# A fused attention and mixture-of-experts kernel: later issue points for the first pass's factors, and the first expert's last 640 tokens cut as 384 and 256

## The chip, the cores and the metric

The kernel runs on one core of a Trainium2 chip (trn2). The metric is the device time in microseconds (us) of one execution of the whole program; lower is better. Its engines run side by side, each through its own queue in order: PE multiplies matrices, DVE, ACT and POOL do elementwise work, SP issues the transfers (DMA).

## The reference

Three layers follow each other. Attention has 4 batches of 8 heads, 576 positions and a mask by blocks of 64. Its output, 2304 tokens of 512 numbers, goes through 8 experts, weighted by a gate whose exponentials are normalised eight times by rows and by columns. The last layer is a dense one with a soft activation and a layer norm.

```python
logits = x @ w_gate
logits = logits - logits.max()
P = np.exp(logits)
for _ in range(8):
    P /= P.sum(1, keepdims=True) + 1e-09
    P /= P.sum(0, keepdims=True) + 1e-09
    P *= N / E
out = np.zeros((N, D), dtype=np.float32)
for e in range(E):
    h = np.maximum(x @ w1[e], 0.0)
    ye = h @ w2[e]
    out += P[:, e:e + 1] * ye
```

## The kernel before

All products are made of pairs of rounded high and low parts, so that one product is three matrix multiplications. The work has these stages:

- **Attention**, up to about 370 us. Products of the first expert (units 0 and 1, half an expert each) are mixed into it as fill. The tokens of the first expert come in segments of 512 and 640; for each block `first_expert` runs the gate (L386 to L396, which writes `logits`), then unit by unit a first layer (L533 to L535, PSUM tile `hps`, from which ACT makes a high half `h` at L539 and DVE a low half at L540) and a second layer (L569 to L571, `yps`). The tiles `hps` and the gate's tiles share two PSUM buffers.
- **The handover**, about 370 to 450 us. The last segment of 640 tokens (`begun`) is still to be done, now in turn with the normalisation of the gate. `sinkhorn` gives ten steps: an exponential (L409), eight rounds (L417 to L431, almost all on DVE, with one small product `cs` at L425 on PE in the middle), and a transposed copy. In the loop of ten, each step is followed by at least 20 units of cost of `begun`. Two steps of `spread_x` (L597 on ACT, L599, L611 to L618) make the sums of token blocks, `X`, for the first pass, and `first_factors(2, ...)` makes the weight factors `W` of unit 2: seven splits, each a cast on ACT (L445) and a subtraction on POOL (L446), and sums of raw weights on DVE (L656, L657, L658, L664).
- **Pass 0**, about 450 to 865 us: units 2 to 15 on the first 768 tokens, with seven products instead of eight for a first layer (`psa`, `psb`, `psc`, L708 to L710; sums at L720, `h` at L750 and L751) and a second layer (L862 to L864, added to `acc` at L868). Each unit also makes the next unit's factors and second weights (`second_weights`, L673, L690 to L700), and from unit 10 on DVE decodes weights of the last layer (L465 to L483).
- **Passes 1 and 2**, to about 1770 us, and then the last layer.

The order of each engine's instructions is not that of the code. A scheduler of the framework takes the place in the code as priority and puts ahead what it thinks could start earlier, so an edit at one place can shift rows hundreds of microseconds later. On the machine each engine then keeps to its list, and a row that waits holds up all rows behind it.

Of the kernel before, what the change touches and what calls it, by code (L numbers as in the profile page):

```python
# [24 lines left out]
def build(ctx, tc, qT, kT, v, w_gate, w1, w1s, w2, w_in, w_out, g_ln, out):  # L25
# [356 lines left out]
    def gate(x, t0, w, t):  # L382

        ps = mm.tile([P, 512], F32, tag="mm", name="gps")
        for n, (c, s) in enumerate([(c, s) for c in range(4) for s in (1, 0)]):
            nc.tensor.matmul(ps[:, 0:w], gw[:, c, :], x[s][:, c, t0 : t0 + w], start=n == 0, stop=n == 7)  # L386
        lt = stg.tile([P, 512], F32, tag="raw", name="glt")[0:64, 0:w]
        nc.scalar.copy(lt, ps[0:64, 0:w])
        yield 9
        pt = mm.tile([P, 4, 64], F32, tag="mm", name="gpt")  # L390
        k = w // P
        for j in range(k):
            nc.tensor.transpose(pt[:, j, :], lt[:, j * P : j * P + P], ident[0:64, 0:64])
        lg = logits[:, t : t + k, :]
        nc.vector.tensor_copy(lg, pt[:, 0:k, 0:E])
        nc.vector.tensor_tensor(lg, pt[:, 0:k, 32 : 32 + E], lg, op=ALU.add)  # L396
        yield 0
# [97 lines left out]
    def load_first(u, pool):  # L495
        e, g = divmod(u, 2)
        wts[u] = ([], [])
        for c in range(4):
            wts[u][0].append(load_weight(pool, w1[e, 4 * g + c]))
            yield 0  # L500

    def load_second(u, pool):
        e, g = divmod(u, 2)
        for c in range(4):
            wts[u][1].append(load_weight(pool, w2[e, (4 * g + c) * P : (4 * g + c + 1) * P, :]))
            yield 0
# [131 lines left out]
    def first_factors(u, stg):  # L638

        e, g = divmod(u, 2)  # L640
        W = {}

        def split(i, a):
            t = weight_tile()
            split_weights(t, a)
            nc.sync.dma_start(fdram[u - 2, int(i) - 1], r32(t))
            W[i] = by_halves(t)

        raw = {}
        for i, k in ((1, 1), (2, 1), (2, 2), (1, 2)):  # L650
            raw[i, k] = stg.tile([P, 512], F32, tag="raw", name="raw")
            nc.sync.dma_start(raw[i, k], w1s[e - 1, g, i - 1, k - 1])
        a11, a12, a21, a22 = raw[1, 1], raw[1, 2], raw[2, 1], raw[2, 2]
        s1 = stg.tile([P, 512], F32, tag="s1", name="s1", bufs=1)
        split("1", a11)
        nc.vector.tensor_tensor(s1, a21, a22, op=ALU.add)  # L656
        nc.vector.tensor_tensor(a21, a11, a21, op=ALU.subtract)  # L657
        nc.vector.tensor_tensor(a11, s1, a11, op=ALU.subtract)  # L658
        split("6", a11)
        split("2", a12)  # L660
        split("7", a21)
        split("5", s1)
        split("4", a22)
        nc.vector.tensor_tensor(a12, a12, a11, op=ALU.subtract)  # L664
        split("3", a12)
        return W
# [212 lines left out]
    def woven(job, other, first, every):  # L879

        for i, cost in enumerate(job):
            yield cost
            if i >= first and (i - first) % every == 0:
                next(other, None)
        run(other)

    def first_expert(seg, tile0, u, v):

        x = xseg[seg]
        blocks = ((0, 512),) if seg == 0 else ((0, 256), (256, 384))  # L890
        for t0, w in blocks:
            yield from gate(x, t0, w, tile0 + t0 // P)
        for i, (t0, w) in enumerate(blocks):
            job = moe(u, x, t0, w, tile0 + t0 // P, "first")
            if i == len(blocks) - 1:
                yield from woven(job, load_first(v, w1p), 17, 3)
            else:
                yield from job
        for i, (t0, w) in enumerate(blocks):
            job = moe(v, x, t0, w, tile0 + t0 // P, "second")  # L900
            yield from woven(job, load_second(v, w1p), 2, 3) if i == 0 else job


    fills = [
        [12, 12 + 9, 9, (1 for _ in load_unit(0, w1p))],
        [44, 80, 200, first_expert(0, 0, 0, 1)],
        [80, 116, 270, first_expert(1, 4, 1, 0)],
        [116, 157, 200, first_expert(0, 9, 0, 1)],
    ]
    done = [0] * len(fills)  # L910
# [30 lines left out]
    W = None  # L941
    for i in range(10):
        next(rounds)
        if i in (1, 5):
            next(spreading)
        if i == 3:
            W = first_factors(2, stg2)
        cost = 0
        while cost < 20:
            cost += next(begun, 20)  # L950
# [231 lines left out]
```

## Time and profile before

| | us |
|---|---|
| median of 3 runs | 1983.65 |
| lowest and highest run | 1982.28, 1986.76 |
| profiled execution, its own time | 1983.74 |
| its span in the trace | 1982.0 |
| PE busy | 1898.4 |
| DVE busy | 1454.0 |
| POOL busy | 1163.6 |
| ACT busy | 743.3 |

The span is the stretch that the trace covers; 1.7 us of the execution's own time lie around it. Busy time of PE counts a pipelined matrix multiplication up to its modelled end. A row of a timeline gives a start, a duration, the engine, the line, the operation, the tiles (out<-in), the shape and, in brackets, how long the engine had been idle before it and who ended that.

### The profile page before, as it was taken

The numbers are of one execution on the slowest core, as the hardware profiler recorded it, in microseconds if no ns is written. First come the engines' busy times: TensorE is split into PE (matmuls) and PEld (weight loads), VectorE is DVE, ScalarE is ACT, GpSimd is POOL, SyncE is SP. The second block draws the span as 40 slices with busy tenths as digits, with TensorE's granted clock in tenths as the row PEclk, the third lists the DMA queues.
The fourth block names the chain that finished last, engine by engine and source line by source line (L and its number), as shares of the span: only waits on it lengthen the run. The fifth ranks groups of instructions, "written<-read, shape, count | busy, mean of one in ns | idle before, by whom it ended". The sixth has DMA issues, their size and how long they took to land.

```text
span 1982.0 us, 31143 instructions
## 1 busy us (share of the span) xinstructions
PE 1898.4 (96%) x10487; PEld 1762.7 (89%) x10487; DVE 1454.0 (73%) x3104; ACT 743.3 (38%) x1555; POOL 1163.6 (59%) x920
## 2 busy tenths in 40 slices
PE   5899999889999999999999999998999999989999
PEld 4688998788998989889999999987999999978887
DVE  5868677666777769888867667797866766678774
ACT  5766657433434434343222222222222122224332
POOL 7775645455766667656666676668757557631000
PEclk8999999999999999999999999998999999989999
DMA  8765554337888888879787787876788787851100
GB/s 233 189 181 150 153 148 117 134 99 270 298 303 309 292 315 311 297 251 370 271 289 265 272 279 257 288 259 238 282 285 294 257 278 274 307 205 44 47 28 32
DMA packets 197758, 454.61 MB, mean 229 GB/s; under 512 B 20432, under 2 KB 78432, under 8 KB 197472
## 3 DMA queue, kind: packets, MB, share of 16 engines
q1 hardware_dynamic: 197600, 452.63, 67.3%
q8 instruction: 84, 1.38, 0.3%
q14 instruction: 74, 0.61, 0.1%
HBM read 295.72 MB, written 128.52 MB: 214 GB/s over the span
## 4 chain that ended last, share of the span: by engine, by line
PE 77%; DVE 9%; DMA 4%; POOL 4%; issue 3%; ACT 1%; SPq 1%; DVEq 0%; POOLq 0%; ACTq 0%
PE yps L708 5%; PE yps L710 5%; PE yps L709 5%; PE psb L709 4%; PE psb L708 4%; PE psb L710 4%; PE yps L862 3%; PE yps L864 3%; PE yps L863 3%; PE psc L710 2%; PE psc L708 2%; PE psc L709 2%; PE psa L708 2%; PE psa L710 2%; PE psa L709 2%
## 5 line engine op out<-in xcount | busy, mean ns | idle before, releaser
L770 POOL TENSOR_TENSOR hf<-hb,hf 128x768 fp32r<-128x768 f32 x196 | 368.4, 1895 | 94.9 <-ACT hf L769 94.9
L769 ACT CAST hf<-hb 128x768 fp32r<-128x768 f32 x196 | 160.5, 836 | 490.4 <-POOL hb L773 158.5
L708 PE MATMUL yps<-hf,W 128*128 128x384 f32 x784 | 268.1, 342 | 10.5 <-DVE hb L762 8.2
L709 PE MATMUL yps<-hf,W 128*128 128x384 f32 x784 | 267.1, 341 | 0.0
L710 PE MATMUL yps<-hf,W 128*128 128x384 f32 x784 | 263.8, 341 | 0.0
L773 POOL TENSOR_TENSOR hb<-hb 128x768 f32<-128x768 f32 x84 | 158.8, 1891 | 161.6 <-DVE hb L762 160.1
L816 DVE TENSOR_TENSOR acc<-yps,acc 128x384 f32<-128x384 f32 x364 | 192.6, 549 | 67.6 <-PE yps L710 66.9
L446 POOL TENSOR_TENSOR w<-raw,w 128x512 fp32r<-128x512 f32 x96 | 125.8, 1323 | 109.3 <-ACT w L445 104.6
L708 PE MATMUL psb<-X,W 128*128 128x384 f32 x504 | 169.7, 337 | 1.4 <-ACT acc L814 1.4
L709 PE MATMUL psb<-X,W 128*128 128x384 f32 x504 | 169.3, 336 | 0.0
L710 PE MATMUL psb<-X,W 128*128 128x384 f32 x504 | 167.7, 335 | 0.0
L708 PEld LDWEIGHTS yps<-hf,W 128*128 128x128 f32 x784 | 149.0, 190 | 13.1 <-DVE hb L762 9.8
L709 PEld LDWEIGHTS yps<-hf,W 128*128 128x128 f32 x784 | 149.1, 190 | 0.0
L720 DVE TENSOR_TENSOR u<-psb,r 128x384 f32<-128x384 f32 x168 | 91.1, 550 | 79.1 <-PE psb L710 71.4
L710 PEld LDWEIGHTS yps<-hf,W 128*128 128x128 f32 x784 | 148.7, 190 | 0.0
L862 PE MATMUL yps<-w,h 128*128 128x512 f32 x336 | 133.3, 397 | 5.5 <-DVE acc L868 2.7
L233 POOL TENSOR_SCALAR e<-e,sv 128x128 f32<-128x128 f32 (+2 forms) x144 | 81.1, 567 | 95.6 <-DVE sv L229 31.4
L446 POOL TENSOR_TENSOR W<-raw,W 128x512 fp32r<-128x512 f32 x84 | 117.7, 1416 | 29.7 <-ACT W L445 29.7
L864 PE MATMUL yps<-w,h 128*128 128x512 f32 x336 | 132.6, 395 | 0.0
L863 PE MATMUL yps<-w,h 128*128 128x512 f32 x336 | 132.5, 394 | 0.0
L1102 POOL TENSOR_SCALAR lh<-ln 128x1024 f16<-128x1024 f32 x18 | 19.1, 1059 | 187.4 <-DVE ln L1099 65.2
L708 PE MATMUL psa<-X,W 128*128 128x384 f32 x336 | 113.5, 338 | 2.9 <-ACT W L445 1.5
(233 smaller groups left out, 5330.5 us busy)
## 6 DMA issues: line engine op xcount, KB each, us to landing
W<-fd SPq DMA_DIRECT2D x392, 512.0 KB, 5.6
fd<-W SPq DMA_DIRECT2D x154, 512.0 KB, 5.2
fd<-w SPq DMA_DIRECT2D x84, 256.0 KB, 4.7
raw<-in_w1s SPq DMA_DIRECT2D x56, 256.0 KB, 5.5
raw<-in_w SPq DMA_DIRECT2D x14, 1024.0 KB, 6.9
raw<-in_w SPq DMA_DIRECT2D x40, 256.0 KB, 3.4
kh<-khigh SPq DMA_DIRECT2D x64, 144.0 KB, 2.9
kl<-kraw SPq DMA_DIRECT2D x64, 144.0 KB, 2.7
```

Source lines behind the costliest of these rows:

```text
L446: nc.gpsimd.tensor_tensor(t[:, 1, :], raw, r32(t[:, 0, :]), op=ALU.subtract)
L708: nc.tensor.matmul(ps, wh, xl, start=start and kc == 0, stop=False, skip_group_check=True)
L709: nc.tensor.matmul(ps, wh, xh, start=False, stop=False, skip_group_check=True)
L710: nc.tensor.matmul(ps, wl, xh, start=False, stop=stop and kc == 1, skip_group_check=True)
L720: nc.vector.tensor_tensor(to, bank[g, a], tmp[g, "r1" if a == "b" else name[1:]], op=ALU.add)
L769: nc.scalar.copy(hi, a)
L770: nc.gpsimd.tensor_tensor(lo, a, r32(hi), op=ALU.subtract)
L773: eng.tensor_tensor(o, a, b, op=ALU.subtract)
L816: nc.vector.tensor_tensor(a, ps, a, op=ALU.add)
L862: nc.tensor.matmul(ps, hl, ws[c][:, 0, :], start=c == 0, stop=False)
L863: nc.tensor.matmul(ps, hh, ws[c][:, 1, :], start=False, stop=False)
L864: nc.tensor.matmul(ps, hh, ws[c][:, 0, :], start=False, stop=c == 3)
```

## The change

Two places of the code differ. In the loop of ten, the two steps of `spread_x` follow the steps numbered 3 and 6 instead of 1 and 5, and `first_factors(2, ...)` step 4 instead of 3. In the last segment (whose first tile is 13) the 640 tokens are cut as 384 and 256 instead of 256 and 384; the segment that begins at tile 4 keeps the old cut.

```diff
     def first_expert(seg, tile0, u, v):
 
         x = xseg[seg]
-        blocks = ((0, 512),) if seg == 0 else ((0, 256), (256, 384))
+
+        blocks = ((0, 512),) if seg == 0 else ((0, 256), (256, 384)) if tile0 == 4 else ((0, 384), (384, 256))
...
     W = None
     for i in range(10):
         next(rounds)
-        if i in (1, 5):
+        if i in (3, 6):
             next(spreading)
-        if i == 3:
+        if i == 4:
             W = first_factors(2, stg2)
         cost = 0
```

The first place where the rows differ is the handover. On ACT, after the gate's copy of the last block (`glt`), these are the rows before, up to the first `h`, which is the high half of the segment's first `hps`:

```order
L388 COPY glt_4923<-gps_4914 64x384
L445 CAST W_5184<-raw_5175 128x512
L597 CAST X1_5030<-b11_5037 128x384
L539 ACTIVATE h_4974<-hps_4961 128x256
L597 CAST X2_5032<-b21_5041 128x384
```

And the same rows now:

```order
L388 COPY glt_4924<-gps_4915 64x256
L445 CAST W_5191<-raw_5182 128x512
L597 CAST X1_5097<-b11_5104 128x384
L597 CAST X2_5099<-b21_5108 128x384
L597 CAST X3_5103<-b22_5110 128x384
L445 CAST W_5198<-raw_5182 128x512
L445 CAST W_5202<-raw_5188 128x512
L445 CAST W_5206<-raw_5184 128x512
L445 CAST W_5210<-s1_5190 128x512
L445 CAST W_5214<-raw_5186 128x512
L597 CAST X7_5100<-t3_5112 128x384
L539 ACTIVATE h_4974<-hps_4961 128x384
```

The first `h` stood behind one cast of `X` and now stands behind four of `X` and six of `W`. On DVE, these are rows of the second normalisation round before, between its first row sum and its column sum (`s1_5881` and `raw_5875` belong to the factors of unit 3):

```order
L417 TENSOR_REDUCE rowt_5016<-pr_99 128x18
L418 TENSOR_SCALAR rowt_5016<-rowt_5016 128x18
L419 RECIPROCAL rowr_5017<-rowt_5016 128x18
L656 TENSOR_TENSOR s1_5881<-raw_5875,raw_5877 128x512
L420 TENSOR_TENSOR pr_99<-pr_99,rowr_5017 128x144
L657 TENSOR_TENSOR raw_5875<-raw_5873,raw_5875 128x512
L423 TENSOR_REDUCE colt_5018<-pr_99 128x8
```

And the same round now, with the row ahead of it:

```order
L540 SCALAR_TENSOR_TENSOR h_5036<-hps_5023,h_5036 128x384
L417 TENSOR_REDUCE rowt_4997<-pr_99 128x18
L418 TENSOR_SCALAR rowt_4997<-rowt_4997 128x18
L656 TENSOR_TENSOR s1_5881<-raw_5875,raw_5877 128x512
L419 RECIPROCAL rowr_4998<-rowt_4997 128x18
L657 TENSOR_TENSOR raw_5875<-raw_5873,raw_5875 128x512
L420 TENSOR_TENSOR pr_99<-pr_99,rowr_4998 128x144
L423 TENSOR_REDUCE colt_4999<-pr_99 128x8
```

The two factor sums (L656, L657) are still in round two; each stands one row earlier, and a low half `h` has come in ahead.

The second place is the start of pass 0 on PE, where unit 3's first product (`psa` with `W_5882`) begins. Before it came directly behind unit 2's last first-layer product:

```order
L708 MATMUL psc_5821<-X3_5036,W_5212 128x384
L709 MATMUL psc_5821<-X3_5036,W_5212 128x384
L710 MATMUL psc_5821<-X3_5036,W_5212 128x384
L708 MATMUL psa_6045<-X1_5030,W_5882 128x384
L709 MATMUL psa_6045<-X1_5030,W_5882 128x384
```

Now second-layer products of unit 2 stand between:

```order
L710 MATMUL psc_5821<-X3_5103,W_5219 128x384
L864 MATMUL yps_5970<-w2_5705,h_5790 128x512
L862 MATMUL yps_5955<-w2_5710,h_5840 128x512
L863 MATMUL yps_5955<-w2_5710,h_5840 128x512
L864 MATMUL yps_5955<-w2_5710,h_5840 128x512
L862 MATMUL yps_5970<-w2_5710,h_5840 128x512
L863 MATMUL yps_5970<-w2_5710,h_5840 128x512
L864 MATMUL yps_5970<-w2_5710,h_5840 128x512
L708 MATMUL psa_6045<-X1_5097,W_5882 128x384
```

From the end of the first expert to this row there were 12 products of the second layer (L862 to L864), and there are 18 now.

The third place is unit 14 on DVE. `h_9506` is the low half that unit 14's second layer needs for its first sums over `psb`. Before, rows of a decode (`a64`, `b64`) stood ahead of it:

```order
L720 TENSOR_TENSOR psb_9423<-psb_9423,r1_9412 128x384
L465 TENSOR_SCALAR a64_9308<-w64_9306 128x256
L474 TENSOR_SCALAR b64_9309<-w64_9306 128x256
L720 TENSOR_TENSOR psb_9432<-psb_9432,r1_9421 128x384
L468 SCALAR_TENSOR_TENSOR a64_9308<-w64_9306,a64_9308 128x256
L720 TENSOR_TENSOR psc_9475<-psc_9475,u2_9430 128x384
L471 SCALAR_TENSOR_TENSOR a64_9308<-w64_9306,a64_9308 128x256
L720 TENSOR_TENSOR psc_9487<-psc_9487,u2_9439 128x384
L477 ISA a64_9308<-a64_9308,b64_9309 128x512
L751 SCALAR_TENSOR_TENSOR h_9506<-psb_9423,h_9506 128x384
```

Now the decode's first row comes behind all four low halves of the unit:

```order
L720 TENSOR_TENSOR psb_9423<-psb_9423,r1_9412 128x384
L751 SCALAR_TENSOR_TENSOR h_9496<-vu3_9494,h_9496 128x384
L698 TENSOR_TENSOR raw2_9265<-s2_9285,raw2_9265 128x2x256
L720 TENSOR_TENSOR psb_9432<-psb_9432,r1_9421 128x384
L751 SCALAR_TENSOR_TENSOR h_9506<-psb_9423,h_9506 128x384
L720 TENSOR_TENSOR psc_9475<-psc_9475,u2_9430 128x384
L700 TENSOR_TENSOR raw2_9265<-raw2_9265 128x2x256
```

In exchange, decode rows now stand ahead of the corresponding low half in units 11, 13 and 15: four rows (L465, L474, L468, L471) in unit 11, three in unit 13 and, between the sum of `psb` and the low half, two (L468, L471) in unit 15, where they stood behind or elsewhere before.

## Rows read from the trace of the kernel before

**Rows 1.** The page's head: span, and busy time of each engine.

```profile
span 1982.0 us, 31143 instructions
...
PE 1898.4 (96%) x10487; PEld 1762.7 (89%) x10487; DVE 1454.0 (73%) x3104; ACT 743.3 (38%) x1555; POOL 1163.6 (59%) x920
```

**Rows 2.** Busy time by stretch; PEclk is the clock granted, 0.50 being half.

```profile
395.00:400.00 5.00, 1.36 (x12) 1.16 (x10) 4.96 (x5) 1.12 (x3) 5.00 (x5) 0.88 1.02 390
400.00:405.00 5.00, 4.41 (x18) 4.41 (x19) 3.80 (x12) 1.75 (x4) 2.33 (x3) 0.50 0.52 169
...
410.00:415.00 5.00, 2.97 (x24) 2.79 (x23) 4.28 (x12) 1.83 (x4) 4.43 (x4) 1.00 0.43 130
...
470.00:475.00 5.00, 5.00 (x16) 4.08 (x17) 4.07 (x8) 3.68 (x7) 3.54 (x4) 0.66 0.99 289
```

**Rows 3.** Whom PE waited for from 345 to 520: total, times, longest.

```profile
PE cs L425 <- DVE colt L423: 6.3, 2, 4.2
PE hps L533 <- DVE h L540: 3.4, 3, 1.4
PE psa L708 <- ACT W L445: 1.5, 1, 1.5
```

**Rows 4.** PE's timeline in the handover.

```profile
376.87 0.39 PE L533 MATMUL hps<-xl,w 128*128 128x256 f32 x1
...
387.16 0.44 PE L533 MATMUL hps<-xl,w 128*128 128x384 f32 x1 [1.39 <-DVE h L540]
...
391.26 0.34 PE L535 MATMUL hps<-xh,w 128*128 128x384 f32 x1
391.57 0.39 PE L425 MATMUL cs<-colt,ones 128*128 128x8 f32 x2
391.82 0.36 PE L569 MATMUL yps<-h,w 128*128 128x256 f32 x1
...
396.08 0.28 PE L571 MATMUL yps<-h,w 128*128 128x256 f32 x1
400.59 0.60 PE L425 MATMUL cs<-colt,ones 128*128 128x8 f32 x2 [4.23 <-DVE colt L423]
```

**Rows 5.** ACT's timeline in the handover.

```profile
379.63 0.38 ACT L539 ACTIVATE h<-hps 128x256 fp32r<-128x256 f32 x1
...
385.01 0.51 ACT L597 CAST X<-t 128x384 fp32r<-128x384 f32 x1
385.43 0.38 ACT L539 ACTIVATE h<-hps 128x256 fp32r<-128x256 f32 x1
```

**Rows 6.** DVE's timeline in the second round: the factor sums of unit 3.

```profile
396.00 1.53 DVE L656 TENSOR_TENSOR s<-raw 128x512 f32<-128x512 f32 x1
...
398.47 1.75 DVE L657 TENSOR_TENSOR raw<-raw 128x512 f32<-128x512 f32 x1
```

**Rows 7.** POOL's timeline: the last low half of the tokens.

```profile
374.43 0.87 POOL L344 TENSOR_TENSOR xl<-xr,xh 128x320 fp32r<-128x320 f32 x1 [2.02 <-ACT xh L343]
```

**Rows 8.** The chain that ended last, from 448 to 475: start, duration, what.

```profile
449.68 6.62 DMA raw<-in_w
...
457.13 5.06 POOL w L446 x4
...
468.33 0.53 ACT W L445
468.90 0.45 PE psa L708
...
474.04 0.23 PE yps L863
```

**Rows 9.** Unit 14: PE's and DVE's timelines, then windows as in group 2.

```profile
852.34 0.50 PE L862 MATMUL yps<-w,h 128*128 128x512 f32 x1 [2.45 <-DVE h L751]
...
851.75 0.54 DVE L751 SCALAR_TENSOR_TENSOR h<-psb,h 128x384 fp32r<-128x384 f32 x1
...
852.00:854.00 2.00, 1.66 (x5) 1.31 (x6) 2.00 (x3) 0.46 (x1) 2.00 (x2) 0.70 1.03 422
854.00:856.00 2.00, 2.00 (x7) 1.81 (x6) 2.00 (x4) 1.99 (x5) 2.00 (x3) 0.50 1.05 426
```

## Prediction, made before the run

> **What bounds the kernel now.** I read the page's head first: PE is busy 1898.4 of 1982.0 us [rows 1], so nothing but PE's idle time and its slow stretches can be won. The change alters no width or count of PE's work in sum, since 384 and 256 columns are the same 640 either way. So I asked where PE waits or runs slow near the rows that the change moves. The list of PE's waits for 345 to 520 us names three [rows 3]: the small product of a normalisation round waits for DVE's column sum (6.3 us, two times), the first layer's `hps` wait for the low half `h` that frees their buffer (3.4 us, three times), and unit 3's first product waits for its factor's cast (1.5 us). The windows show what the long one costs twice: after 4.23 us of idle [rows 4] the granted clock is 0.50 from 400 to 405 us [rows 2], the 1.2 GHz level, so that PE, which restarts at 400.59, does half work for at least 4.4 us and loses some 2.5 us. After the shorter wait of the two (6.3 - 4.2 = 2.1 us, within 410 to 415) the clock stays 1.00. In 470 to 475 it is 0.66 on average [rows 2]: at 0.50 for 5 x 0.34 / 0.5 = 3.4 us, 1.7 us lost, behind the wait of 1.5. Further on one more place matters, unit 14: PE waits 2.45 us there and runs at 0.70 and 0.50 afterwards [rows 9], that is half clock for 1.2 + 2.0 us, 1.6 us lost.
>
> **What the change does there.** The diff says "later". The rows of the order say something else, so I cost what they show.
>
> *The factor sums in round two.* L656 and L657 took 1.53 and 1.75 us on DVE, inside the 9.0 us between the two `cs` [rows 4, 6]; they are why the column sum was late, with 36 products at (396.08 - 391.82) / 35 = 0.12 us as PE's only cover, 4.3 us. They belong to unit 3, not unit 2, and in the changed order they stand in the same round. So this term is not removed. The round gains the low half of a relu on DVE (0.5 us, the size of its like in unit 14 [rows 9]) and its cover becomes 12 products of 384 columns and 24 of 256: at (391.26 - 387.16) / 23 = 0.18 and 0.12 us, 5.0 us instead of 4.3. Wait: 9.0 + 0.5 - 5.0 = 4.5 against 4.2 to 4.5 now. Nil.
>
> *The gate of the last tokens.* The first block now ends at column 384, and columns from 320 on get their low half only at 374.43 + 0.87 = 375.30 [rows 7]. Block one was through the gate earlier; now both come behind that time, each with a product, a copy and a transpose: I count 375.4 for the last two products of 384, 0.5 for ACT's copy, 0.3 for the transposes, 1.0 for the eight products of 256, 0.5 and 0.3 again: the first layer starts near 378.5 instead of 376.87 [rows 4]. That is 1.6 us late.
>
> *The first relu.* It ran at 379.63, behind one cast of `X`; the cast of `X7` ran at 385.01 [rows 5]. The relu now stands behind that one. Two relus fewer are ahead of it, so it starts near 385.2. A relu's start at 385.43 let PE go at 387.16 [rows 4, 5], 1.7 us later, so PE restarts at about 386.9, after an idle time from 378.5 + 24 x 0.18 + the small products = 383.2: 3.7 us in one piece, where it had 3.4 in three. It then needs 24 x 0.18 = 4.3 us to the first `cs`, 391.2, the column sum included about 391.6 as before. But by then it has done 48 x 0.18 = 8.6 us of first-layer work instead of 48 x 0.12 + 24 x 0.18 = 10.1: 1.5 us behind, which holds the gate's 1.6 already. The following rounds give back part: round four's wait of 2.1 has 5.0 us of cover now instead of 24 x 0.12 = 2.9, or is longer by one or two relus of 0.5; I take 0.9 back. Handover in all: +0.6, with bounds. Below: if PE's lateness lets round two's sums find POOL idle, they are shorter (L656 has 0.68 to 1.85 us in the trace, half of the pair's 3.3 us to be won) and with a wait near 2.7 the clock keeps up: 0.6 - 1.7 - 2.5 = -3.6. Above: the clock falls in the 3.7 us too: +3.1. That one stands between 2.1, after which it held, and 4.23, after which it fell.
>
> The Trainium skill (TensorE: Matmul & The Clock Gate, section Why this matters for your kernels) speaks against the change here: it says that an idle gap between bursts of products sends the array back to the half rate. Rows agree for the long wait and not for the one of 2.1 us, and they show half clock after only 1.5 us at 470. By the rule the handover costs 3.1 us, by the rows 0.6.
>
> *Start of pass 0.* Unit 3's first product hung on a chain that starts with the last product of the first expert: load 6.62, POOL's splits, DVE's sums, ACT's cast of `W` at 468.33, product at 468.90 [rows 8]. Six more second-layer products stand ahead of it now, 6 x 0.23 = 1.4 us of work [rows 8], of the 1.5 that PE waited. The chain itself keeps its members; with relus exchanged against the sums it may be 0.5 longer or shorter. What is left of the wait is 0 to 0.7; whether the clock then still falls is open (0 to 1.7). Taken: -1.2 - 0.8 = -2.0, bounds 0 and -3.2.
>
> *Unit 14.* `h_9506` ended at 851.75 + 0.54 and PE started 0.05 later [rows 9]. Five decode rows that stood ahead of it are gone behind the unit's low halves; one of the second weights' sums has taken their place. Gone: 2.45 + 1.6 = 4.1 us. Where the decode went: ahead of the like low half in units 11, 13 and 15. In units 11 and 13 PE has the same second-layer and next-unit work between as in unit 14, and three or four decode rows against five; in unit 15 only the twelve products of `psc` (2.1 us after the second `psb`), against a sum, a decode row and a relu of about 0.5 each. I put 1.0 us back for the three. -3.1, bounds -4.1 and +8.2 (three waits like the one removed, less that one).
>
> *The rest.* SP's list moves four token loads of pass 1 ahead of three weight loads of unit 0; those weights are multiplied more than 10 us later, and if this cover went, the cost would be up to one load, 6.6 us [rows 8]. Taken: nil. Before 365 us the rows are the same. Behind pass 0 rows are exchanged at the pass's ends only. Nil.
>
> **Sum**: 0.6 - 2.0 - 3.1 = -4.5 us on the profiled execution's 1983.74 (span 1982.0), which stands at the median of the runs, 1983.65: **1979.2 us**.
>
> **Rivals.**
> *The change does what it says:* round two loses its 4.2 us of wait and the 2.5 of clock. For it: the issue point is later. Against it: L656 and L657 are still there. 1983.7 - 6.7 - 2.0 - 3.1 = 1971.9.
> *The clock falls before the first relu* (the rule named above goes this way): 1979.2 + 2.5 = 1981.7. For it: 3.7 is nearer 4.23 than 2.1. Against it: less of PE's work depends on when PE gets there, since round two waits for DVE anyhow.
> *The waits only move:* DVE's load at unit 14 and the chain at 468.9 stay as long, and the new orders pay what the old did: 1983.7 + 0.6 = 1984.3. For it: DVE is the engine that is late in both and has the same rows to do. Against it: the cover counted above.
> *Slower: the decode is ahead in three units instead of one.* Each of units 11, 13 and 15 pays 4.1 like unit 14 did, and the start of pass 0 gives its 2.0: 1983.7 + 0.6 - 2.0 + 8.2 = 1990.5. It decides from two such units on (+4.1 against -2.0 and +0.6: 1986.4). For it: unit 13's cover is the same as unit 14's was. Against it: its decode rows ahead are three, not five.
>
> **How the numbers follow.** A measurement of this kernel tells about 0.2% (4 us) from no change: faster means under 1979.7, slower over 1987.6. My forecast has 0.45 (its own range 1976 to 1982.5), the change as named 0.10, the clock 0.16, waits that move 0.13, three decodes 0.16. Of the forecast's 0.45, three quarters lie under 1979.7: 0.34; with the 0.10 and a little of the clock's, 0.46 faster. Slower is the last rival, 0.15. The rest, 0.39, is the same. The range is 1974.5 to 1987.5: it leaves out half of the change as named and most of the three decodes.
>
> **What would show it.** In the changed profile: the first relu (L539) of the last segment at about 385 behind the cast of `X7`; one idle time of PE of 3 to 4 us ahead of 387; L656 and L657 between two `cs` 9 us apart, with a PE wait over 3 us; no or a short wait at unit 3's first product and a clock of 1.00 from 470 to 475; no wait of 2 us at unit 14's second layer. Wrong would be: a first `cs` far from 391.6; waits of over 1 us in units 11, 13 or 15; a difference that comes from passes 1 and 2, where I expect none.

## The result, and the profile after

The kernel got slower: 2002.38 us median of 6 runs (1998.14 to 2006.04) against 1983.42 of 6 (1981.41 to 1986.76), a ratio of 1.0094 with a 95% interval of 1.0079 to 1.0109. The forecast was 1979.2. The profiled execution took 2004.37 us, 20.6 more than the one of before. These are its page's head rows, the answer to [rows 1]:

```profile
span 2002.6 us, 31141 instructions
...
PE 1908.7 (95%) x10487; PEld 1771.4 (88%) x10487; DVE 1448.5 (72%) x3104; ACT 742.0 (37%) x1555; POOL 1154.3 (58%) x920
```

PE is busy 10.3 us longer on the same 10487 products, at a granted clock of 0.979 on average instead of 0.985, so more of them ran at half clock; and it is idle 10.3 us longer. DVE and POOL do no more than before.

**Where the time went.** I laid the two traces side by side by PE's work: for a moment of the trace before, the moment at which PE in the other trace had multiplied as many columns in all its matmul rows. The difference is how late it is. It is -0.9 at 340 us, ahead of the first changed row, -1.1 at 500, +2.2 at 740, +7.5 at 880, +16.4 at 980 and still +16.4 at 1260, +20.6 at the end. So the handover and the start of pass 0, where the forecast put two of its three terms, cost nothing together. Some 8 us went in units 3 to 15, and 9 from 880 to 980, 7 of these at the start of pass 1 between 904 and 912. Unit 15's wait falls behind 880 too, but the trace before has waits of 1.1 and 0.8 us there which the new one lacks, so that unit adds under 1 us.

**The handover.** Whom PE waited for from 345 to 520 us, as in [rows 3]:

```profile
PE hps L533 <- DVE h L540: 3.4, 2, 2.9
PE gps L386 <- POOL xl L344: 2.8, 1, 2.8
PE cs L425 <- DVE colt L423: 2.1, 1, 2.1
```

Rows of the timelines of ACT, DVE and PE there, which answer to [rows 4 to 6]:

```profile
386.55 0.51 ACT L597 CAST X<-t 128x384 fp32r<-128x384 f32 x1
386.96 0.48 ACT L539 ACTIVATE h<-hps 128x384 fp32r<-128x384 f32 x1
389.07 0.45 PE L533 MATMUL hps<-xl,w 128*128 128x384 f32 x1 [2.94 <-DVE h L540]
394.94 0.28 PE L425 MATMUL cs<-colt,ones 128*128 128x8 f32 x2
398.43 0.68 DVE L656 TENSOR_TENSOR s<-raw 128x512 f32<-128x512 f32 x1
402.41 0.39 PE L425 MATMUL cs<-colt,ones 128*128 128x8 f32 x2 [2.07 <-DVE colt L423]
470.90 0.34 PE L708 MATMUL psa<-X,W 128*128 128x384 f32 x1
```

The first relu does stand behind the cast of `X7`, but at 386.96 and not 385.2, and the first `cs` comes at 394.94 instead of 391.6. The second round gives half of that back: L656 finds POOL idle and takes 0.68 us instead of 1.53, the two `cs` are 7.5 us apart and not 9.0, and PE waits 2.07 instead of 4.23. Round four gives back nearly all the rest: its `cs` waits 0.58 us instead of 2.03. Unit 3's first product (470.90) no longer waits. These are windows of that stretch, as in [rows 2]; the trace before shows 1.00 in the first three of them:

```profile
375.00:380.00 5.00, 3.98 (x16) 2.95 (x16) 0.64 (x4) 1.36 (x3) 0.27 (x1) 0.50 0.05 8
380.00:385.00 5.00, 5.00 (x21) 4.94 (x21) 2.10 (x5) 2.50 (x6) 2.43 (x3) 0.68 0.93 318
...
390.00:395.00 5.00, 5.00 (x23) 5.00 (x21) 4.57 (x6) 1.62 (x3) 5.00 (x5) 0.66 0.76 278
...
470.00:475.00 5.00, 5.00 (x27) 4.57 (x26) 4.26 (x8) 3.12 (x7) 3.54 (x3) 1.00 0.81 254
```

So PE ran at half clock behind the 2.8 us that the gate's first block waits for the last tokens' low half, and again behind the 2.94 us.

**Units 11, 13 and 15.** The longest group of PE's waits from 740 to 900 us:

```profile
PE yps L862 <- DVE h L751: 7.5, 3, 2.7
```

Before, that line read 2.4 us, once (unit 14, [rows 9]). Unit 14 has no such wait now; units 11, 13 and 15 have one each. Timelines of PE for the three, of DVE and POOL for unit 13, and of DVE for unit 15:

```profile
758.59 0.71 PE L862 MATMUL yps<-w,h 128*128 128x512 f32 x1 [2.30 <-DVE h L751]
826.75 0.62 PE L862 MATMUL yps<-w,h 128*128 128x512 f32 x1 [2.46 <-DVE h L751]
892.81 0.50 PE L862 MATMUL yps<-w,h 128*128 128x512 f32 x1 [2.70 <-DVE h L751]
...
822.16 0.90 DVE L465 TENSOR_SCALAR a<-w 128x256 uint32<-128x256 uint32 x1
822.98 1.38 DVE L474 TENSOR_SCALAR b<-w 128x256 uint32<-128x256 uint32 x1
824.28 1.48 DVE L468 SCALAR_TENSOR_TENSOR a<-w,a 128x256 uint32<-128x256 uint32 x1
...
826.15 0.54 DVE L751 SCALAR_TENSOR_TENSOR h<-psb,h 128x384 fp32r<-128x384 f32 x1
...
821.62 3.87 POOL L446 TENSOR_TENSOR W<-raw,W 128x512 fp32r<-128x512 f32 x3 [1.80 <-DMA fd<-W]
...
890.41 0.28 DVE L474 TENSOR_SCALAR b<-w 128x256 uint32<-128x256 uint32 x1
...
891.08 0.41 DVE L468 SCALAR_TENSOR_TENSOR a<-w,a 128x256 uint32<-128x256 uint32 x1
```

In unit 13 the three decode rows in front of the low half take 0.90 + 1.38 + 1.48 = 3.8 us while POOL subtracts; in unit 11 it is the same with four rows. In unit 15 it is not: POOL has no row from 890 to 892, and the four decode rows there take 0.28 + 0.28 + 0.41 + 0.41 = 1.4 us, among sums of pass 1's token blocks (L599). The clock behind the first two waits is 0.50 for 3.4 us each, behind the longest it stays 1.00 (windows of units 11, 13 and 15):

```profile
760.00:762.00 2.00, 2.00 (x7) 1.72 (x6) 1.97 (x6) 0.80 (x2) 1.28 (x1) 0.50 1.04 424
...
826.00:828.00 2.00, 1.25 (x3) 0.97 (x4) 2.00 (x4) 0.86 (x2) 2.00 (x2) 0.74 1.03 402
828.00:830.00 2.00, 2.00 (x7) 1.69 (x6) 2.00 (x4) 1.00 (x2) 0.72 (x2) 0.50 1.03 422
...
890.00:892.00 2.00, 0.11 (x1) 0.00 (x0) 2.00 (x7) 0.81 (x3) 0.00 (x0) 1.00 0.89 241
...
894.00:896.00 2.00, 2.00 (x12) 1.92 (x12) 2.00 (x6) 1.16 (x3) 0.00 (x0) 1.00 1.02 418
```

**The start of pass 1.** The two longest of PE's waits from 900 to 1000 us (before, one of 1.4 us for ACT's copy was the longest there):

```profile
PE psa L708 <- ACT acc L814: 3.1, 1, 3.1
PE psa L708 <- DVE hb L762: 2.8, 1, 2.8
```

The chain that ended last shows whom the second of them waited for. `pb` holds the gate's weights for a pass, by which DVE scales the hidden rows `hb`:

```profile
913.97 0.32 SPq L607
...
914.34 7.56 DMA pb<-pd
...
921.93 0.57 DVE hb L762
...
922.54 0.69 PE psa L708
```

`pb` lies where pass 0's hidden rows lay, so its load waits for the last product of pass 0's second layer. PE's last such row starts at 911.65 and ends at 912.05. The load is issued at 914.34, behind a token load (L607) that waited for one of DVE's sums of token blocks (L599), and DVE, ready at 917.80, is idle for 4.1 us. In the trace before the same three rows are:

```profile
901.22 0.40 PE L864 MATMUL yps<-w,h 128*128 128x512 f32 x1
...
901.65 0.96 SPq L822 DMA_DIRECT2D pb<-pd  x2
...
911.61 1.01 DVE L762 SCALAR_TENSOR_TENSOR hb<-psa,pb 128x384 f32<-128x384 f32 x2
```

There 10.4 us lay between the last second-layer product and DVE's first use. Now 30 of the first products of pass 1 stand ahead of that last product where 13 did, and DVE is ready 6 us behind it, less than the load takes. The wait of 3.1 us hangs on a decode piece; DVE's, ACT's and PE's timelines:

```profile
949.22 1.48 DVE L465 TENSOR_SCALAR a<-w 128x256 uint32<-128x256 uint32 x1
...
960.39 0.42 DVE L483 SCALAR_TENSOR_TENSOR f<-b,a 128x256 f32<-128x256 uint32 x1
...
960.84 0.40 ACT L445 CAST w<-f 128x256 fp32r<-128x256 f32 x1 [7.07 <-DVE f L483]
961.15 2.76 ACT L814 COPY acc<-yps 128x384 f32<-128x384 f32 x7
...
962.06 0.44 PE L708 MATMUL psa<-X,W 128*128 128x384 f32 x1 [3.10 <-ACT acc L814]
```

One piece's seven rows hold DVE for 11.6 us, ACT's cast waits for them, and behind the cast stand the copies that free PE's bank.

### The profile page after: what moved, and what is told of

Read it like the earlier page. It is cut to its first block, busy times and chain, and to the rows that moved or that the text cites. A ratio compares the mean times of both kernels' runs of the same rounds, so it can differ in the third digit from the quotient of the medians.

```text
span 2002.6 us, 31141 instructions
## 1 busy us (share of the span) xinstructions
PE 1908.7 (95%) x10487; PEld 1771.4 (88%) x10487; DVE 1448.5 (72%) x3104; ACT 742.0 (37%) x1555; POOL 1154.3 (58%) x920
## 3 DMA queue, kind: packets, MB, share of 16 engines
q8 instruction: 84, 1.38, 0.3%
## 4 chain that ended last, share of the span: by engine, by line
PE 72%; DVE 10%; DMA 7%; issue 4%; POOL 4%; ACT 2%; SPq 1%; POOLq 0%; ACTq 0%; DVEq 0%
PE yps L708 6%; PE yps L710 6%; PE yps L709 6%; PE psb L710 3%; PE psb L709 3%; PE psb L708 3%; PE yps L862 2%; PE yps L863 2%; PE yps L864 2%; PE psa L710 2%; PE psa L708 2%; PE psa L709 2%; PE psc L708 2%; PE psc L709 2%; PE psc L710 2%
## 5 line engine op out<-in xcount | busy, mean ns | idle before, releaser
L446 POOL TENSOR_TENSOR w<-raw,w 128x512 fp32r<-128x512 f32 x96 | 130.0, 1368 | 111.1 <-ACT w L445 109.0
L720 DVE TENSOR_TENSOR u<-psb,r 128x384 f32<-128x384 f32 x168 | 91.6, 551 | 89.4 <-PE psb L710 88.7
L862 PE MATMUL yps<-w,h 128*128 128x512 f32 x336 | 133.0, 397 | 11.3 <-DVE h L751 9.2
L864 PE MATMUL yps<-w,h 128*128 128x512 f32 x336 | 132.2, 394 | 0.0
```

The costliest lines, as they stand in the source:

```text
L446: nc.gpsimd.tensor_tensor(t[:, 1, :], raw, r32(t[:, 0, :]), op=ALU.subtract)
L720: nc.vector.tensor_tensor(to, bank[g, a], tmp[g, "r1" if a == "b" else name[1:]], op=ALU.add)
L862: nc.tensor.matmul(ps, hl, ws[c][:, 0, :], start=c == 0, stop=False)
L864: nc.tensor.matmul(ps, hh, ws[c][:, 0, :], start=False, stop=c == 3)
```

## The experiments

Lateness of PE by work against the kernel before, gained in each stretch (us, worked out as above from each run's profile; a minus is time won). Two traces of the same lists, before and e1, differ by 2.7 in the first column and by 0.7 at most in the others. That is not the whole spread: e5, e13 and e14 have the rows of after up to 906 us, and from 740 to 880 the four show +5.3 to +9.7.

| | to 340 | 340-500 | 500-740 | 740-880 | 880-980 | 980-end |
|---|---|---|---|---|---|---|
| after | -0.9 | -0.2 | +3.3 | +5.3 | +8.9 | +4.2 |
| e1 | +2.7 | -0.7 | 0.0 | +0.1 | 0.0 | -0.5 |
| e2 | +1.0 | +0.3 | 0.0 | +0.8 | -0.7 | +2.7 |
| e3 | +2.1 | +9.0 | +7.6 | +7.1 | +6.9 | +0.9 |
| e4 | -0.9 | -4.8 | -0.6 | -0.7 | +5.0 | +1.0 |
| e5 | -0.9 | +0.5 | +3.8 | +9.7 | +1.6 | +1.6 |
| e6 | +1.7 | -4.5 | -0.7 | -0.4 | +3.3 | +1.4 |
| e7 | -0.1 | +0.4 | +4.1 | -1.4 | +15.6 | +3.0 |
| e8 | -1.5 | -0.3 | -0.1 | -4.8 | +9.4 | +3.7 |
| e9 | +1.2 | -1.1 | +0.1 | -4.8 | -3.6 | +24.1 |
| e10 | +0.7 | -1.3 | +0.1 | -4.8 | -4.3 | +31.0 |
| e11 | -0.9 | +0.9 | +3.8 | -3.2 | -6.1 | +31.2 |
| e12 | +2.2 | -5.5 | -0.7 | -4.1 | -3.7 | +27.5 |
| e13 | -0.6 | -1.3 | +4.1 | +6.5 | +4.6 | +0.3 |
| e14 | -0.4 | -1.2 | +4.0 | +8.5 | -4.2 | +3.8 |
| e15 | -0.8 | -1.7 | +0.1 | -1.9 | -3.1 | +2.5 |
| e16 | +0.4 | -2.9 | -0.7 | -0.6 | -3.3 | +3.5 |

**Which half of the change?** e1 is the later issue points with the old cut.

```diff
-        if i in (1, 5):
+        if i in (3, 6):
             next(spreading)
-        if i == 3:
+        if i == 4:
             W = first_factors(2, stg2)
```

> The later issue points alone, with the old cut 256 and 384. Every engine's list of rows is that of the kernel before, row for row (only the numbers in tile names differ). Theory 1 (the change is the cut alone; a call that stands one step later in the code moves no row): 1983 us, ratio 0.999 to 1.001, and a PE that waits 4.2 us for the second round's column sum as before. Rival (the issue points are what cost the 19 us, or part of it): 1990 to 2002, ratio 1.003 to 1.009.

Measured: 1985.34 us, ratio 1.0008 (0.9997 to 1.0018), and 4.26 us of wait for the second `cs`. The half of the change that the title names first does nothing: the lists of all five engines are those of before, row for row. So the sentence ahead of the prediction, that the place in the code is the scheduler's priority, does not hold for these calls. Only the cut moves rows. All runs below keep the old issue points, so "on after" means with the new cut; e5, e13 and e14 show the rows of after on PE, DVE, ACT and POOL up to 906 us, so that with the new cut the issue points move no row until then either.

**The cut, or the order behind it?** The scheduler settles into one of a few orders for pass 0. With other amounts of work of the last segment behind each normalisation step the old cut gets the order of after, and the new cut that of before or a third one. All three have the old issue points and differ in one more number:

```diff
         cost = 0
-        while cost < 20:
-            cost += next(begun, 20)
+        while cost < 24:
+            cost += next(begun, 24)
```

(24 in e2 and 28 in e4, on the new cut; 12 in e3, on the old.)

> The new cut 384 and 256, with at least 24 instead of 20 units of cost of the last segment behind each normalisation step. With it the lists of rows behind the handover are those of the kernel before again: in units 11 to 15 the decode rows ahead of the unit's first two low halves over psb are 0+0, 0+3 (unit 12), 0+0, 5+4 (unit 14), 0+0, and pass 1 starts in the old order. Theory 1 (the loss comes from where rows stand in units 9 to 15 and at the start of pass 1, and the new cut's handover costs nothing or gains 1 to 2 us): 1980 to 1985, ratio 0.998 to 1.001, a PE wait of some 2.4 us in unit 14 and none over 1 us in units 11, 13, 15. Theory 2 (the cut itself costs, by the handover): 1995 to 2003, ratio 1.006 to 1.010.

> The old cut 256 and 384 and the old issue points, with at least 12 instead of 20 units of cost of the last segment behind each normalisation step. With it the lists of rows behind the handover are those of the changed kernel: 4+5 decode rows ahead in unit 11, 3+4 in unit 13, 2+2 in unit 15, and pass 1 starts in the changed kernel's order. Theory 1 (the places of the rows behind the handover): 1997 to 2005, ratio 1.007 to 1.011, PE waits of 2.3 to 2.7 us in units 11, 13 and 15, and the second block's weights (pb) landing after DVE has asked for them. Theory 2 (the cut itself): 1982 to 1987, ratio 0.999 to 1.002.

> The new cut with at least 28 instead of 20 units of cost behind each step: a third order behind the handover. Decode rows ahead of the two low halves over psb: 0+2 in unit 11, 0+2 in unit 13, none in units 12, 14 and 15; pass 1's token sums have 15 decode rows among them, and the first load of pb stands ahead of the last decoded rows' store. Theory 1, with decode rows ahead of a unit's first low half as the cause in pass 0: no PE wait over 1 us in units 11 to 15, so unit 14's 4 us are gone too; the start of pass 1 may still cost what it costs in the changed kernel (8): 1977 to 1990. Theory 2 (the cut): 1995 to 2003.

Measured: e2 1983.68 us, ratio 1.0000 (0.9989 to 1.0011); e3 2011.91, 1.0147 (1.0126 to 1.0169); e4 1984.24, 1.0003 (0.9993 to 1.0012). PE's waits from 740 to 1000 us, of e2 and then of e3:

```profile
PE psb L708 <- ACT acc L814: 1.4, 1, 1.4
PE yps L862 <- DVE h L751: 1.0, 1, 1.0
```

```profile
PE yps L862 <- DVE h L751: 8.0, 3, 2.9
PE psa L708 <- ACT acc L814: 3.5, 1, 3.5
PE psa L708 <- DVE hb L762: 2.0, 1, 2.0
```

From 500 to 1000 us e2 has the rows of before on PE, DVE, ACT and POOL, and e3 those of after but for three of PE's. The waits follow the order, not the cut. Unit 14's wait in e2 is 1.0 us where 2.4 was expected. That e3 is slower than after, and than its theory, comes for the most part from its handover: with 12 units of cover PE waits 8.6 us for one column sum, and the stretch to 500 costs 9.0. e4's handover, with the most cover, waits for no column sum at all and wins 4.8; then the start of pass 1 takes 5.0 back. In unit 15 it waits 1.7 us for a low half, where its theory had no wait over 1.

**pb.** e5 (on after) and e6 (on e4) give `pb` a space of its own, so that it is loaded in the handover.

```diff
+    pbp = ectx.enter_context(tc.tile_pool(name="pbp", bufs=2, side="left"))
     fctx = ExitStack()
...
-    pbp = ectx.enter_context(tc.tile_pool(name="pbp", bufs=2, side="left"))
```

> The changed kernel with the tiles of the gate's weights (pb) in a space of their own, so that their loads for pass 1 are issued in the handover (some 400 us) and no longer stand behind token loads on SP's list at the end of pass 0. Units 11, 13 and 15 keep their decode rows ahead. Theory (at the start of pass 1, pb that lands at 921.9 makes DVE idle for 4.1 us and PE wait 2.8 us at half clock behind it): PE is 8 us behind the kernel before at the end of pass 0 as it is now, and 6 to 9 us less behind than now from 980 us on; 1993 to 1998 us, ratio 1.005 to 1.007. Rival (DVE, with its decode rows among the token sums, is what is late, and pb only comes last): PE waits as long for the token sums or for hb, 2000 to 2004 us, ratio 1.008 to 1.010.

> The new cut with 28 units of cost behind each step (as in the run of that name), and pb's tiles in a space of their own as well. Theory (pb's late landing costs 3.4 us of PE wait and the clock behind it there): the lag of +8 us that came between 900 and 940 us is gone, and with the 6 us that its handover and units 11 to 15 had won: 1975 to 1980 us, ratio 0.996 to 0.998. Rival (DVE is late by itself): 1983 to 1985 us, ratio 0.999 to 1.001.

Measured: e5 1999.28 us, ratio 1.0079 (1.0058 to 1.0100); e6 1981.43, 0.9989 (0.9977 to 1.0002). In e5 the stretch from 880 to 980 costs 1.6 instead of 8.9, as the theory says, but units 11 to 15 came out 4 us worse than in after on the same rows, so its time lies between the two expectations. In e6 the wait for `hb` went, and one of 2.8 us for ACT's copies came at 945; its time lies between theory and rival.

**No decode in pass 0**, on after (e7) and on before (e8):

```diff
-        if 8 <= n < 40:
-            decode(*late[n - 8])
+        if n >= 14:
+            k = n - 14
+            for m in ((2 * k, 2 * k + 1) if k < 4 else (k + 4,)):
+                if m < 32:
+                    decode(*late[m])
```

> The changed kernel with no decode in pass 0: all 32 pieces of it are done in passes 1 and 2, two at a time for its first four places. Theory (decode rows ahead of a unit's first low half are what makes PE wait in units 11, 13 and 15): no PE wait for a low half over 1 us in these units, and PE, which is now 2 us ahead of the kernel before at 580 us and 8 us behind at 870, is not behind it at 870. Rival (the new order of the units' own rows is the cause, with or without the decode): waits of over 2 us stay, and it is 8 us behind at 870. The time in all can't be told, since the decode goes elsewhere: 1985 to 2000 us by the theory.

> The kernel before with no decode in pass 0, as in the run beside it. Theory: unit 14's wait of 2.45 us and the 1.6 us of slow clock behind it are gone, so that PE is 4 us ahead of the kernel before at 890 us, and what then is left between this run and the one beside it is the handover (1 to 2 us for the new cut) and the start of pass 1. Rival (the order of the units' own rows): this run is 8 to 10 us ahead of the one beside it at 870 us.

Measured: e7 2004.13 us, ratio 1.0104 (1.0085 to 1.0123); e8 1992.96, 1.0045 (1.0028 to 1.0063). PE's waits in e7 from 740 to 900 us:

```profile
PE yps L862 <- DVE h L751: 1.4, 2, 0.8
PE psa L710 <- POOL W L446: 0.9, 2, 0.4
PE yps L862 <- DVE acc L868: 0.7, 1, 0.7
```

The waits of over 2 us are gone, unit 15's too, so decode rows have a part in all three; that e7's time is over what the theory gave comes from the start of pass 1. But the rival is right in part: at 880 e7 is 3.0 behind and e8 6.7 ahead, 9.7 apart as the rival had it, and 8 when their starts are taken off. The new order of the units' own rows costs by itself: in the trace of after from 500 to 740, where no decode row stands yet, 2.1 us (three waits of 0.4 for POOL's part of a factor, one of 0.8 for a low half), where before had none. Behind 740 the waits above, 3.0 us, point the same way, but this is no clean test, because taking the decode away also moves some of the units' own rows: 102 of PE's from 740 to 900 in e7, 322 in e8. At the start of pass 1, where two pieces of decode stand for each unit, both runs lose 9 to 16 us.

**The decode later still**: from unit 6 of pass 1 on, two pieces for each of ten units. e9 is before with it, e10 with pb's space too, e11 is after with both, e12 e4 with both.

```diff
-        if 8 <= n < 40:
-            decode(*late[n - 8])
+        if n >= 18:
+            k = n - 18 + min(max(n - 20, 0), 10)
+            for m in (k, k + 1) if 20 <= n < 30 else (k,):
+                if m < 32:
+                    decode(*late[m])
```

> The kernel before with the whole decode moved behind the start of pass 1: its 32 pieces begin at unit 6 of pass 1, two for each unit from unit 8 of pass 1 to unit 3 of pass 2, and end at unit 13 of pass 2. Theory (decode rows cost PE time only at the end of pass 0 and in the first units of pass 1, where DVE and POOL are both full; from 1000 to 1250 us DVE has 13 to 17 of 50 us free): unit 14's 4 us and the waits of the first units of pass 1 (1.45 us and the like) go, PE is 6 to 9 us ahead of the kernel before at 980 us and keeps it: 1974 to 1979 us, ratio 0.995 to 0.998. Rival (the decode costs the same wherever it stands): what is won until 980 us is lost until 1400 us, 1982 to 1990 us, ratio 0.999 to 1.003.

> The run beside it (old cut, decode from unit 6 of pass 1 on) with pb's tiles in a space of their own too. Theory: in this order pb's loads stand behind token loads as in the changed kernel, so that 0 to 6 us more are won at 900 to 940 us: 1970 to 1978 us, ratio 0.993 to 0.997. Rival (nothing waits for pb there): as the run beside it within 2 us.

> The changed kernel (new cut, later issue points) with both suspected costs taken away: the decode from unit 6 of pass 1 on, and pb's tiles in a space of their own. Theory (these two are the whole loss, and the new cut with its order is worth nothing by itself): its time is that of the old cut with the same two edits within 4 us, 1970 to 1980 us, ratio 0.993 to 0.998; no PE wait over 1 us in units 11, 13, 15. Rival (the order that the new cut makes of the units' own rows costs by itself): 8 us or more behind the old cut with the same edits.

> The new cut with 28 units of cost behind each step (a handover that was 5 us shorter in the run of that name), the decode from unit 6 of pass 1 on, and pb's tiles in a space of their own: meant to beat both kernels. Theory: 5 us from the handover, 4 from unit 14's decode and 0 to 4 from the start of pass 1: 1969 to 1977 us, ratio 0.993 to 0.997. Rival (what is won early is lost again to waits at the start of pass 1 and at 1300 to 1400 us, as 6 of the 8 us were in the run with pb alone): 1979 to 1984 us, ratio 0.998 to 1.000.

Measured: e9 1999.06 us, 1.0076 (1.0061 to 1.0092); e10 2000.81, 1.0090 (1.0072 to 1.0108); e11 2010.56, 1.0132 (1.0114 to 1.0151); e12 1999.04, 1.0076 (1.0053 to 1.0099). All four times are beyond what theory or rival gave in numbers. Until 980 the theory holds: all four win time from 740 on, e11 as well, whose loss there is gone. Behind it two pieces a unit cost 24 to 31 us. Between the runs the rivals are right: e10 is within 2 us of e9, so `pb` costs that order nothing, and e11 is 9.8 behind e10. The profiled runs show 4.3 of that, and from 500 to 880 alone +0.6 against -4.7, which points at the units' own order again. PE's waits in e9 from 1000 to 1400 us, the two longest groups:

```profile
PE psa L708 <- DVE acc L816: 9.2, 11, 1.3
PE psb L708 <- DVE u L720: 4.5, 1, 4.5
```

I had read DVE's 13 to 17 idle us in 50 as room for a second piece. One fits, as before shows; the second does not.

**The start of pass 1 alone.** No decode for units 2 and 3 of pass 1, the later pieces moved by two units, one each (e13, on after); with pb's space too (e14); both on before (e15) and on e4 (e16).

```diff
-        if 8 <= n < 40:
-            decode(*late[n - 8])
+        if 8 <= n < 14 or n >= 16:
+            m = n - 8 if n < 14 else n - 8 - 2
+            if m < 32:
+                decode(*late[m])
```

> The changed kernel with no decode for units 2 and 3 of pass 1; the pieces that stood there and all later ones come two units later, one for each unit. Units 11, 13 and 15 keep theirs. Theory (the PE wait of 3.1 us at 962 hangs on a decode piece: its seven rows take 1.9 us each on DVE, and ACT's cast of it stands ahead of the copies that free PE's bank): that wait is under 1.5 us, PE's lag at 980 us is 12 to 14 us instead of 16.4, and 1996 to 2000 us, ratio 1.006 to 1.008. Rival (the products' sums by themselves are late): the wait stays, 2000 to 2004 us.

> The run beside it with pb's tiles in a space of their own as well: of the 10 us that the changed kernel loses between 900 and 980 us both suspected causes are taken away, and the three units at the end of pass 0 are left as they are. Theory: the lag does not rise by more than 2 us between 900 and 980; 1990 to 1996 us, ratio 1.003 to 1.006. Rival (a third cause): it rises by over 4 us.

> The kernel before with the same two edits (no decode for units 2 and 3 of pass 1, pb in a space of its own). Theory: its start of pass 1 has little to win, 1.45 us of wait at 948 and nothing for pb: 1980 to 1984 us, ratio 0.998 to 1.000. Rival (the two edits are worth as much here): 1974 to 1978 us.

> The new cut with 28 units of cost behind each step, pb in a space of its own, and no decode for units 2 and 3 of pass 1: one piece for each unit elsewhere, since two for each unit cost 24 us between 1080 and 1400. Meant to beat both kernels. Theory (its handover wins 5, its units 11 to 15 wait for no low half, and with pb and the decode out of the way the start of pass 1 no longer gives 5 back): 1973 to 1979 us, ratio 0.995 to 0.998. Rival (the loss moves on once more): 1980 to 1984 us.

Measured: e13 1999.84 us, ratio 1.0080 (1.0053 to 1.0107); e14 1995.33, 1.0057 (1.0037 to 1.0077); e15 1981.40, 0.9982 (0.9969 to 0.9995); e16 1979.76, 0.9971 (0.9959 to 0.9983). PE's waits from 900 to 1000 us, of e5 (pb alone) and then of e13 (pause alone); e14 has none over 0.1:

```profile
PE psa L708 <- ACT acc L814: 2.7, 1, 2.7
PE psc L708 <- DVE X L599: 0.9, 1, 0.9
```

```profile
PE psa L708 <- DVE hb L762: 4.5, 1, 4.5
```

Each edit takes its own wait away and leaves the other. The stretch costs +8.9 with neither, +1.6 and +4.6 with one, -4.2 with both; before itself goes to -3.1. No third cause is needed there. All four came as the theory had it, but for e16's time, 0.8 us over its range, and a wait of 1.7 us for a low half that it keeps in unit 15. e16 beats both kernels (1984.83 is the median of before beside it), and the start of pass 1 no longer takes its handover's gain back. But e15, the old cut with the same two edits, is only 1.6 us behind it and their ten runs each overlap: that the new cut adds to the gain is not shown.

## Why the prediction was wrong, step by step

*Factor sums in round two, gate, first relu* (+0.6, bounds -3.6 to +3.1) *and the start of pass 0* (-2.0): -1.4 forecast, -0.2 measured. The parts came otherwise than drawn, and that the two sums lie so near is luck. The step that failed is the clock, to which the sum gave nothing in the handover: it fell behind the gate's wait, for which the sum had 1.6 us of time and no clock, and behind the 2.94 us that PE waits for the first relu's low half, which was the rival that I gave 0.16. Everything up to the first `cs` was 3.3 later than I had it. The second round gave back half of it by what I had named as the lower bound, sums that find POOL idle, and round four, where I took 0.9 back, the rest. That -2.0 was won at the start of pass 0 is right within half a microsecond: from 460 to 500 us PE's lateness falls from +1.3 to -1.1. Of this the clock, 1.00 from 470 to 475 instead of 0.66, is 1.7 and the wait the smaller part, since PE now waits 0.9 us for a low half just ahead.

*Unit 14* (-4.1): right. Its wait is gone, and e8, which takes the decode away from the old order, wins 4.8 from 740 to 880.

*"I put 1.0 us back for the three"*: this step failed. I counted rows, three or four against five, where [rows 9] and the rows between showed durations. Three rows in unit 13 take 3.8 us; the five in unit 14 before took 0.28 + 0.28 + 1.10 + 1.04 + 1.02 = 3.7. A row's cost hung on POOL being busy beside it, and the cover was, as I had written, the same as in unit 14. By that alone units 11 and 13 had to wait like unit 14. The three wait 2.30, 2.46 and 2.70 us, with 1.7, 1.7 and 0 for the clock (half of the time at 0.50): 10.9. This was the rival that I gave 0.16 ("decode ahead in three units"), and its 4.1 a unit was nearly right in the first two. That unit 15 waits as well is luck for that rival: four short rows of 1.4 us in all, beside an idle POOL, do not explain 2.70 by themselves, and which of the other rows ahead of that low half makes the rest stays open.

*The order of the units' own rows*, for which the sum has no term, costs 2.1 us of PE's waits until 740, where +3.3 were lost, and in e7, without the decode, another 3.0 behind it. These 3.0 are not to be added to the 10.9: in after PE's waits from 740 to 900 are the three above and two for `acc` (2.1 us, 2.7 before). I had looked only at places where a decode row moved.

*"Behind pass 0 rows are exchanged at the pass's ends only. Nil."* This is the dearest step that failed: +8.9 us from 880 to 980. The exchange puts more of pass 1's first products ahead of pass 0's last second-layer products, and so takes the cover off a load that cannot be issued before the last of these. With pb's space 7.3 of the 8.9 go (e5), with the decode's pause 4.3 (e13). I had looked at SP's list for a load that stands earlier or later, and not at what releases one.

*Passes 1 and 2*: 0 from 980 to 1260, as forecast, and +4.2 behind it. Between 980 and the end e2, with nearly before's order in passes 1 and 2, shows +2.7 and e1 -0.5; how much of the 4.2 belongs to the new order I leave open.

The Trainium skill (TensorE: Matmul & The Clock Gate, section Why this matters for your kernels) says that an idle gap between bursts of products sends the array back to the half rate. It speaks of longer gaps than the three of units 11, 13 and 15; half clock stood behind two of these all the same, and not behind the longest, 2.70 us.

What the runs do not settle is why the scheduler goes from one order to another when a cut or a cover changes. They show that it does, and that the time follows the order.

## What to carry to other kernels

Compare the built lists before costing an edit: here half of the change moved no row, and the other half moved rows for 500 us behind its place. Cost a moved row by its duration in its new neighbourhood, not by its count, and at a stage's end ask of each load what frees its space and how much work lies between that and its first use. When a change wins or loses by the order it happens to get, try a neighbouring number (24 or 28 here) before judging the idea.

## What the runs showed of the hardware that I had not expected

The decode's DVE rows, whose operands all lie in SBUF (the engines' working memory), are several times longer while POOL works. In the trace after, from 700 to 1900 us, the decode's L474 has a median of 0.29 us in 26 rows with POOL idle and 1.38 in 5 with POOL busy throughout, L468 0.42 in 23 and 1.49 in 8. A sum with a PSUM operand (L720) takes 0.56 in both cases (159 and 126 rows). One piece of decode so costs DVE some 2.5 us, the sum of its seven rows' medians with POOL idle, or 11.6 as at 949.22. The Trainium skill (SBUF — State Buffer, section Who interferes with whom) says why: a DVE row with two SBUF inputs or in a two-port mode shares a port pair with a GpSimd (POOL) row that reads SBUF, and the second to come is blocked until the first is done. The rows of L468, with two inputs in SBUF, and of L720, with one of its two in PSUM, agree; whether L474, with a single input, is in such a mode no run shows.

The same wait at the same row can cost the clock or not: in unit 15 the window behind 2.70 us of idle PE shows 1.00 in the trace after, and behind 2.69 us in e13 the clock is 0.50 from 894 to 896.
